# A batch-wise order for VectorE, a 32x32 q sketch with the Gram-weighted columns and FFN groups cut to batch 0, in a polysketch attention and FFN kernel

## The chip, the cores and the metric

One core of a Trainium2 chip. The metric is the device time of one launch in microseconds (us). Before the change the median is 131.13 us (four runs, 130.19 to 131.8). A run is called slow when it is over 1.5% above the fastest run of the same kernel. Ratios use fast runs alone; medians are over all runs.

## The reference, cut to what matters

```python
# q, k, v: (B, H, S, D) = (4, 4, 1088, 32); S1, S2: (8, 32)
phi(x) = outer(S1 x, S2 x)                   # 8 x 8 = 64 features per token and head
kv  = sum_s phi(k)_f v_d;  z = sum_s phi(k)_f
x   = (phi(q) kv) / (phi(q) z + 1e-6)        # 4352 tokens x 128 (heads side by side)
h   = x @ w_in                               # 128 -> 2048
out = (h - tanh(h)) @ w_out                  # 2048 -> 128
```

The FFN needs 160 tiles of tanh (16 per group of up to 512 columns) on ScalarE, and two matmuls per tile on TensorE. Columns are tokens; a batch has 1088 of them. `h @ w_out` without the tanh is folded into one small product, wc = w_in w_out (kept as wch + wcl). A sketch is the pair S1 x and S2 x. The denominator phi(q) z equals S1 q times G (S2 q), where G, the Gram matrix of a head, is the sum over tokens of the outer product of k's two sketches; G (S2 q) gives the Gram-weighted columns.

## The kernel before

A Python program lists operations with a key and their dependences; its own list scheduler models time and so fixes the order of instructions on every engine before the kernel is built.

```python
GCOLS = [256] + [512] * 7 + [384, 128]       # FFN groups: group 2 begins at column 768, inside batch 0
...
    # in schedule(): among what could start within 30 ns of the earliest, the lowest key wins
    t, o = min(((t, o) for t, o in cands if t <= t0 + 30.0), key=lambda x: (x[1].key, x[0]))
    ...
    st = max(t + 1400.0, dma_free)           # one model for all DMA queues
    dma_free = st + o.dma / 285.0
    o.t1 = dma_free + 600.0
...
    # q_side(): the key of a q transpose comes from when its columns are due, not from its batch
    P.add(_v((z - a) * 32), ... e.transpose(qT...), key=max(key, col_time(b * S + a * 32) - 9000) - 2000)
    # q sketch: S1 and S2 by 8 matmuls of 64x32, the Gram-weighted one by 4 of 128x32
    for g in range(4):
        for rh in range(2):
            e.matmul(psa4[g*32:(g+1)*32, rh, 0:sn], wab.ap[rh*64:(rh+1)*64, :], ...)
    ...                                       # two transposes back to abq
    e.matmul(psa4[g*32:(g+1)*32, 3, 0:sn], sc.ap[:, :], ...)
    ...                                       # one transpose back to cq
    # batch 0 in three sketches and pieces, the others in one sketch and two pieces
    q_side(b, sc, kvb, [(0, 2), (2, 5), (5, 9)], [(0, 2), (2, 5), (5, 9)], k0 + 5000)   # b == 0
    q_side(b, sc, kvb, [(0, 9)], [(0, 5), (5, 9)], kd + 6000)                            # others
```

Where the scheduler sees a long gap on TensorE early in the kernel, it puts filler matmuls on zeros there (line 367). Names on VectorE (DVE): kT and qT are 32x32-block transposes of loaded k and q; abk, abq, cq, abc bring a sketch back from PSUM; w and qp are the outer products; qpT transposes qp for the last attention product num; ot transposes an FFN group's output. The tiles psa, psh and pso are in PSUM, where the matmuls put their results; kvd and kvb are copies of the kv product out of PSUM, with a transpose on TensorE between them; xT is the attention's output, the FFN's input; th is a tile of tanh.

## Time and profile before

| view | what it shows |
|---|---|
| page, busy shares | PE 86%, ACT 65%, DVE 55% of a 130.5 us span |
| windows 50 to 104 us | PE busy 51.2 of 54 us |
| windows 104 to 127 us | ACT busy 22.8 of 23 us |
| windows 30 to 40 us | PE busy 2.6 of 10 us, ACT 0.8 |

The page's picture of the span in 40 slices (3.26 us each; a digit is a tenth busy):

```profile
PE   6998989674048899899899999999999999999990
DVE  5368678496934969963728982641997201002010
ACT  0315822751014269578587899659789999999990
PEclk9999999999855699999999999999999999999999
DMA  2999999999700000040000410400040130401322
```

The dip at 30 to 37 us is what the change aims at. The granted clock is 0.5 from 34.7 to 44.9 us; TensorE has no matmul from 30.97 to 37.12. The same stretch by windows (columns: stretch, its length, busy us and instructions of each engine, granted TensorE clock, DMA share, GB/s):

```profile
30.00:35.00 5.00, 0.83 (x25) 0.34 (x24) 3.90 (x11) 0.10 (x1) 0.00 (x0) 0.97 1.01 203
35.00:40.00 5.00, 1.76 (x72) 1.28 (x81) 2.07 (x4) 0.73 (x3) 0.00 (x0) 0.50 0.10 22
40.00:45.00 5.00, 4.53 (x62) 1.31 (x51) 3.93 (x7) 2.15 (x4) 0.00 (x0) 0.51 0.00 0
```

VectorE's timeline shows why TensorE starved (columns: start, us, engine, line, operation, tiles, count; in brackets the idle time before it and what ended it):

```profile
24.18 0.85 DVE L559 STREAM_TRANSPOSE qT<-qL 128x640 f32<-128x640 f32 x1 [1.02 <-DMA qL<-in_q_dram]
25.77 0.65 DVE L559 STREAM_TRANSPOSE qT<-qL 128x448 f32<-128x448 f32 x1 [0.64 <-DMA qL<-in_q_dram]
...
32.15 0.85 DVE L559 STREAM_TRANSPOSE qT<-qL 128x640 f32<-128x640 f32 x1 [0.73 <-DMA qL<-in_q_dram]
32.92 0.25 DVE L598 TENSOR_TENSOR m<-abq,cq 128x128 f32<-128x128 f32 x1
...
35.77 1.30 DVE L628 STREAM_TRANSPOSE qpT<-qp 128x512 f32<-128x512 f32 x2
```

These 640 and 448 wide qT are those of batches 1 and 2. Batch 0's last piece (m at 32.92, qpT at 35.77) stands behind a q load of batch 2 that landed at 32.1 us: VectorE idles 0.73 us for it, although m's last input, cq, was back at 31.42. ScalarE's timeline dates what follows:

```profile
38.68 0.59 ACT L318 CAST xT<-psa 128x384 bf16<-128x384 f32 x2 [8.59 <-PE psa L636]
39.86 0.60 ACT L702 ACTIVATE th<-psh 128x512 bf16<-128x512 f32 x1 [0.59 <-PE psa L636]
...
54.75 0.69 ACT L318 CAST xT<-psa 128x640 bf16<-128x640 f32 x1 [1.31 <-PE psa L636]
55.92 2.56 ACT L702 ACTIVATE th<-psh 128x512 bf16<-128x512 f32 x5 [0.48 <-PE psh L699]
```

FFN group 1 starts at 39.9 us, and group 2, which needs batch 1's first columns, at 55.9 us.

### The profile page before, as it was taken

How to read it: one execution, taken by the hardware profiler on the slowest of the kernel's cores; microseconds unless marked ns; L12 is line 12 of the kernel's file. 1: busy time of each engine (PE TensorE's matmuls, PEld its weight loads, DVE VectorE, ACT ScalarE, POOL GpSimd, SP SyncE). 2: the span in 40 equal slices, each digit the busy share in tenths (PEclk: the TensorE clock that was granted, in tenths of full speed). 3: DMA queues.
4: the chain of work that ended last, by engine and by line, in shares of the span. 5: the costliest groups of instructions: out<-in, count | busy, mean ns of one | idle time of the engine just before them, and what ended most of it. 6: DMA issues, size and time to landing. Idle time of an engine off the chain costs nothing.

```text
span 130.5 us, 3757 instructions
## 1 busy us (share of the span) xinstructions
PE 111.9 (86%) x1602; PEld 54.7 (42%) x1618; DVE 72.1 (55%) x155; ACT 85.2 (65%) x189; POOL 1.8 (1%) x14
## 2 busy tenths in 40 slices
PE   6998989674048899899899999999999999999990
PEld 4856656341022452333543444453335433334460
DVE  5368678496934969963728982641997201002010
ACT  0315822751014269578587899659789999999990
POOL 4100000000000000000000000000000000000000
PEclk9999999999855699999999999999999999999999
DMA  2999999999700000040000410400040130401322
GB/s 43 287 312 343 337 222 319 209 306 201 166 20 0 0 8 0 5 68 17 0 0 5 65 15 18 68 5 0 0 71 14 28 57 0 70 10 25 61 39 41
DMA packets 25552, 11.28 MB, mean 86 GB/s; under 512 B 19136, under 2 KB 24000, under 8 KB 25536
## 3 DMA queue, kind: packets, MB, share of 16 engines
q1 hardware_dynamic: 24528, 10.44, 35.4%
q10 hardware_dynamic: 1008, 0.61, 1.8%
q8 instruction: 12, 0.20, 0.7%
q14 instruction: 4, 0.03, 0.1%
HBM read 8.81 MB, written 2.23 MB: 85 GB/s over the span
## 4 chain that ended last, share of the span: by engine, by line
PE 48%; SPq 12%; DVE 12%; ACT 11%; DMA 11%; issue 3%
PE pso L712 16%; PE psh L699 16%; SPq L393 12%; DMA qL<-in_q_dram 11%; ACT th L702 10%; PE psa L636 6%; PE psa L532 3%; DVE w L522 3%; PE pso L716 2%; PE psa L491 2%; DVE abk L496 2%; DVE ot L721 1%; DVE qT L559 1%; PE psa L570 1%; ACT xT L318 1%
## 5 line engine op out<-in xcount | busy, mean ns | idle before, releaser
L702 ACT ACTIVATE th<-psh 128x512 bf16<-128x512 f32 (+3 forms) x160 | 72.0, 566 | 10.2 <-PE psh L699 9.3
L699 PE MATMUL psh<-xT,wi 128*128 128x512 bf16 (+3 forms) x152 | 51.9, 353 | 2.7 <-ACT th L702 1.2
L712 PE MATMUL pso<-th,wo 128*128 128x512 bf16 (+3 forms) x154 | 49.3, 349 | 1.1 <-issue 0.5
L699 PEld LDWEIGHTS psh<-xT,wi 128*128 128x128 bf16 x160 | 15.3, 98 | 24.2 <-ACT th L702 14.7
L712 PEld LDWEIGHTS pso<-th,wo 128*128 128x128 bf16 x160 | 15.3, 98 | 19.2 <-ACT th L702 7.0
L721 DVE STREAM_TRANSPOSE ot<-pso 128x512 f32<-128x512 f32 (+3 forms) x10 | 6.3, 635 | 25.7 <-PE pso L712 25.7
L636 PE MATMUL psa<-qpT,kvb 32*32 32x128 f32 (+3 forms) x576 | 10.1, 294 | 6.8 <-DVE qpT L628 6.8
L318 ACT CAST xT<-psa 128x384 bf16<-128x384 f32 (+3 forms) x11 | 5.1, 479 | 14.5 <-PE psa L636 14.5
L367 PE MATMUL pso<-zz 128*128 128x256 bf16 x86 | 12.6, 296 | 1.1 <-DVE zz L366 1.1
L628 DVE STREAM_TRANSPOSE qpT<-qp 128x512 f32<-128x512 f32 (+1 forms) x16 | 11.5, 755 | 0.1
L623 DVE TENSOR_TENSOR qp<-ap,abq 128x512 f32<-128x512 f32 (+1 forms) x16 | 11.3, 744 | 0.2
L522 DVE TENSOR_TENSOR w<-abk 128x768 f32<-128x768 f32 x12 | 11.1, 949 | 0.1
L636 PEld LDWEIGHTS psa<-qpT,kvb 32*32 32x32 f32 x576 | 6.6, 106 | 10.4 <-DVE qpT L628 7.5
L367 PEld LDWEIGHTS pso<-zz 128*128 128x128 bf16 x86 | 8.6, 106 | 3.2 <-DVE zz L366 1.1
L496 DVE STREAM_TRANSPOSE abk<-psa 128x288 f32<-128x288 f32 x8 | 3.4, 459 | 8.1 <-PE psa L491 8.1
L559 DVE STREAM_TRANSPOSE qT<-qL 128x448 f32<-128x448 f32 (+3 forms) x9 | 6.1, 673 | 2.9 <-DMA qL<-in_q_dram 2.9
L532 PE MATMUL psa<-w,vL 128*32 128x64 f32 x288 | 6.5, 223 | 1.2 <-DVE w L522 1.2
L575 DVE STREAM_TRANSPOSE abq<-psa 128x288 f32<-128x288 f32 (+3 forms) x12 | 3.9, 359 | 6.3 <-PE psa L570 6.3
L485 DVE STREAM_TRANSPOSE kT<-kL 128x576 f32<-128x576 f32 (+1 forms) x8 | 5.6, 718 | 3.1 <-DMA kL<-in_k_dram 3.1
L532 PEld LDWEIGHTS psa<-w,vL 128*32 128x32 f32 x288 | 4.7, 110 | 4.2 <-DVE w L522 3.6
L662 ACT CAST wi<-wi_f 128x512 bf16<-128x512 f32 x4 | 2.5, 620 | 4.5 <-DMA wi_f<-in_moe_w_in_dram 4.3
L491 PE MATMUL psa<-kT,wab 64*32 64x288 f32 x64 | 3.4, 481 | 1.3 <-ACT xT L318 1.1
(54 smaller groups left out, 59.1 us busy)
## 6 DMA issues: line engine op xcount, KB each, us to landing
kL<-in_k_dram SPq DMA_DIRECT2D x3, 544.0 KB, 11.9
vL<-in_v_dram SPq DMA_DIRECT2D x9, 144.0 KB, 12.5
wi_f<-in_moe_w_in_dram SPq DMA_DIRECT2D x4, 256.0 KB, 6.2
wo_f<-in_moe_w_out_dram SPq DMA_DIRECT2D x4, 256.0 KB, 7.2
out_dram<-ot SPq DMA_DIRECT2D x16, 64.0 KB, 2.0
qL<-in_q_dram SPq DMA_DIRECT2D x3, 320.0 KB, 13.8
qL<-in_q_dram SPq DMA_DIRECT2D x4, 224.0 KB, 12.7
vL<-in_v_dram ACTq DMA_DIRECT2D x3, 144.0 KB, 3.9
```

Of the source, the lines that this page charges most:

```text
L367: filler = (lambda e, n: e.matmul(bank_o.slots[0][0][:, 0:256], zz.ap[:, 0:128], zz.ap[:, 128:384], start=True, stop=True), zop, bank_o)
L393: return P.add({eng: (430.0, 0.0)}, lambda e, n: e.dma_start(out=o_, in_=i_), w=w, key=key, dma=nbytes)
L522: P.add(_v(768), lambda e, n, p=p, wv=wv: e.tensor_tensor(out=wv.ap.rearrange("p (x i j) -> p x i j", i=8, j=8), in0=abh()[:, 0, p * 12:(p ...
L532: i = e.matmul(psa4[h * 32:(h + 1) * 32, 2, 0:64], vL[b][:, h, blk * 32:(blk + 1) * 32], wv.ap[:, (bi * 4 + h) * 64:(bi * 4 + h + 1) * 64] ...
L559: P.add(_v((z - a) * 32), lambda e, n, a=a, z=z: e.transpose(qT.ap[:, a * 32:z * 32], qL[b][:, a * 32:z * 32]), r=[val], w=[qT], key=max(k ...
L623: P.add(_v(cn * 256), lambda e, n, aq=aq, qp=qp, av=av, c0=c0, c1=c1, cn=cn: e.tensor_tensor(out=qp.ap[:, 0:cn * 256].rearrange("p (x i j) ...
L628: P.add(_v(cn * 256), lambda e, n, qp=qp, qt=qt, c0=c0, c1=c1, cn=cn: e.transpose(qt.ap[:, c0 * 256:c1 * 256], qp.ap[:, 0:cn * 256]), r=[q ...
L636: i = e.matmul(psa4[h * 32:(h + 1) * 32, g, 0:nb * 32], kvb.ap[g * 32:(g + 1) * 32, x, h * 32:(h + 1) * 32], qq[g * 32:(g + 1) * 32, 0:nb, ...
L699: P.add(_pe(n_ / 2.4 + 2.6), lambda e, n, jb=jb, hv=hv: e.matmul(hv.ap[:, 0:n_], wi[jb // 4].ap[:, (jb % 4) * 128:(jb % 4 + 1) * 128], xt, ...
L702: P.add(_a(n_), lambda e, n, hv=hv, th=th: e.activation(out=th.ap[:, 0:n_], in_=hv.ap[:, 0:n_], func=AF.Tanh, scale=-1.0), r=[hv], w=[th], ...
L712: fn = lambda e, n, x=x, st=st, sp_=sp_: e.matmul(ov.ap[:, 0:n_], wo[x // 4].ap[:, x % 4, :], ths[x].ap[:, 0:n_], start=st, stop=sp_)
L721: P.add(_vp(n_), lambda e, n: e.transpose(ot.ap[:, 0:n_], ov.ap[:, 0:n_]), r=[ov], w=[ot], key=-60000)
```

## The change

The intent is that a piece of batch 0 never stands behind work of a later batch on VectorE, with fewer and larger VectorE instructions in the q sketch, and FFN groups cut so that the first three need batch 0 alone. The core of the diff, with cuts:

```diff
-GCOLS = [256] + [512] * 7 + [384, 128]
+GCOLS = [256, 384, 448] + [512] * 6 + [192]
+WINDOW = {"tensor": 60.0, "vector": 150.0, "scalar": 60.0, "gpsimd": 30.0, "sync": 30.0}
 ...
-                t, o = min(((t, o) for t, o in cands if t <= t0 + 30.0), key=...)
+                t, o = min(((t, o) for t, o in cands if t <= t0 + WINDOW[e]), key=...)
 ...
-                st = max(t + 1400.0, dma_free)
-                dma_free = st + o.dma / 285.0
-                o.t1 = dma_free + 600.0
+                st = max(t + 1400.0, dma_free.get(e, 0.0))        # a model per issuing queue
+                dma_free[e] = st + o.dma
+                o.t1 = dma_free[e] + (600.0 if o.key < -89800 else 2000.0)
 ...
-    qcut = {0: [0, 8, 20, 34]}                                    # others [0, 20, 34]
+    qcut = {0: [0, 8, 34]}                                        # others whole
 ...
+    def nk():                                                     # attention keys: program order
+        seq[0] += 1
+        return -50000.0 + seq[0]
 ...
+            for h in range(H):                                    # q sketch: S1 | S2 | Gram-weighted S2
+                for g in range(4):
+                    i = e.matmul(psa4[g * 32:(g + 1) * 32, h, 0:sn], wq[h * 32:(h + 1) * 32, :],
+                                 qv4(b)[h * 32:(h + 1) * 32, s0:s1, g, :], start=True, stop=True)
+        P.add(_pe(sn * 4 / 2.4 + 100), sk, ..., w=bk, key=nk(), mode="32x32")   # all four psa banks
+        P.add(_vp(sn * 4), ... e.transpose(abc ...), r=bk, w=[abc], key=nk())   # one, in place of three
 ...
-                after=[])
+                after=[last], name=f"wc{jb}")                     # wc waits for the last wo cast
 ...
-    for b in range(B):
-        kd = k0 if b == 0 else col_time(b * S) - 16500.0
-        sc, kvb = k_side(b, kd)
-        ...
+    attention_first()                                             # batch 0: sketches (0,2) and (2,9)
+    weights()
+    for b in range(1, B):
+        k_side(b)
+        st = q_front(b)                                           # one sketch, one divide per batch
+        q_back(b, st)
```

Also moved: the PSUM copies gm, sc, kvd, kvb and xT are ScalarE's alone; one wi cast and three wo casts went to GpSimd; the ring of tanh tiles has 24 slots in place of 28.

## The prediction

> **What bounds it now.** The windows show three stages.
> - 0 to 40 us: attention of batch 0, behind DMA and VectorE. From 30 to 40 us TensorE is busy 2.6 of 10 us. VectorE's timeline shows why: it runs in order, and transposes of later batches' q stand ahead of batch 0's last q piece (qT at 24.18, 25.77, 32.15 us, each after a DMA wait). Its xT copy comes at 38.7 us, the first 512-column FFN group's tanh at 39.9. TensorE's clock is 0.5 from 34.7 to 44.9 us.[...]
> - 40 to 104 us: TensorE, busy 9.1 to 9.6 of each 10 us after 50. Group 2 (columns 768 on) waits for batch 1's first xT copy and starts tanh at 55.9.
> - 104 to 127 us: ScalarE, 60 tanh back to back (23.7 us), then a tail of 3.3 us.
>
> **What the change does.**
> 1. VectorE order: batch 0's q pieces no longer stand behind later q. Batch 1's kT still stands ahead of batch 0's second abc; its load landed at 20.5 us and the bytes ahead of it are the same, so VectorE starts again there.
> 2. q sketch: 8 matmuls 64x32 (0.73 us) and 4 of 128x32 (0.65) become 16 in 32x32, estimate 0.8: TensorE saves 0.6 us a batch. Three VectorE transposes (0.85 + 0.44 us) become one of 1152 columns (estimate 1.35): equal. One divide per batch instead of two saves about 0.6 us.
> 3. gm, kvd, kvb, xT all go to ScalarE (0.2 to 0.7 us each); it has room in the middle.
> 4. FFN groups 256, 384, 448 cover batch 0's 1088 columns, so batch 1 is first needed at 1088 instead of 768.
> 5. wo casts mostly on GpSimd; all wc matmuls wait for the last. wo3 landed at 18.0, so group 0 starts near 20.5, before 22.3.
>
> **Timeline expected** (old durations and landings). VectorE from 20.5: kT 0.7, abc 1.1, wcl and divide 1.8, qp and qpT: batch 0 done at 29 (was 37.1). Then kT, qT, abk, w, more kT and qT, abc, divide and five blocks of batch 1, 16.5 us without a DMA wait: 45.7. num 1.2, xT 0.7: group 3 (column 1088) starts near 48. Groups 1 and 2 fill 27 to 43 at ScalarE's pace; ScalarE then waits 5 us, TensorE about 2.5[...].
> From there the old trace is the measure: group 2 started at 55.9 with 3584 columns, batches 2 and 3 and one piece of batch 1 left, and ended (ot) at 127.9: 72.0 us. The new one has 320 columns less (34 matmuls of 0.2155 us per 512: 4.6 us) and 1.2 us less sketch: 66.2. 48 + 66.2 + 2.6 (output) = 116.8; timed runs lie some 0.4 above the profile.
>
> **Predicted: 117 us, 80% between 112 and 122.** Faster by over 2%: 0.95; within 2%: 0.04; slower: 0.01.
>
> **Signs.** Right: num of batch 0's last piece by 30 us instead of 37; no 0.5 clock between 20 and 100 us; group 3 tanh at 46 to 50 us; the ScalarE-bound end near 21 us. Wrong: VectorE waiting for kL or qL after 21 us; ScalarE held by wch.
>
> **What would make it wrong.** [...]kL or wo3 landing later, loads being cut and ordered differently; slow GpSimd casts; or VectorE faster than summed, the gap shrinking (-3 us).

The estimates in it can be followed from the profile before: 512-column matmuls start 0.216 us apart; transposes of 448 and 640 columns take 0.63 and 0.84 us, by which 1152 come to about 1.4; num's 32 matmuls of 32x32 (64 records) take 1.07 us with 128 columns and 1.18 with 160, by which 16 with 288 come to about 0.8 (this last is my reckoning; the record does not say from what 0.8 was taken). The divide of a later batch (m, den, rd, ap) took 2.23 us in two pieces before and takes 1.75 in one after, so it saves 0.5 where 0.6 was forecast.

## The result, and the profile after

| | before | after |
|---|---|---|
| median, us | 131.13 (130.19 to 131.8, 4 runs) | 123.83 (122.75 to 124.78, 4 runs) |
| profiled span, us | 130.5 | 122.6 |
| PE / ACT busy, us | 111.9 / 85.2 | 107.0 / 85.9 |
| first tanh of groups 1, 2, 3 | 39.9, 55.9, 67.8 | 31.8, 43.3, 53.6 |
| first group that needs batch 1 | group 2 (from column 768) | group 3 (from column 1088) |

The ratio is 0.942 (0.9324 to 0.9516). Ratios here are the mean time of one kernel's fast runs over that of the other's fast runs of the same rounds, so not quite the ratio of the medians quoted. The kernel is faster by 7.3 us, where 14 were forecast, and lies above the range of 112 to 122. Both profiled runs were slow ones (132.3 us, a run outside these four, and 124.78 us), so the two profiles are compared like with like.

The page after, same lines (slices of 3.07 us):

```profile
PE   6995696849859999969999999989999999989980
DVE  5529480895738999984908992662999020020210
ACT  0402661746737789777788898838988998989970
PEclk9999679985999999999999999999999999999999
DMA  1999999999991004022000310050005005004052
```

The hole at 30 to 37 us is gone. In its place are smaller dips, and two short falls of the clock, at 13.2 to 16.7 and 26.9 to 30.3 us. By windows:

```profile
25.00:30.00 5.00, 3.41 (x47) 2.21 (x47) 4.08 (x6) 2.92 (x9) 0.00 (x0) 0.69 1.05 230
30.00:35.00 5.00, 3.53 (x114) 1.73 (x82) 3.49 (x5) 2.50 (x6) 0.00 (x0) 0.97 1.07 228
35.00:40.00 5.00, 4.85 (x104) 2.32 (x104) 2.71 (x5) 3.25 (x10) 0.00 (x0) 1.00 0.42 96
```

VectorE's timeline, from the load it waits for to group 3's input:

```profile
21.80 0.78 DVE L502 STREAM_TRANSPOSE kT<-kL 128x576 f32<-128x576 f32 x1 [3.82 <-DMA kL<-in_k_dram]
...
31.39 0.45 DVE L781 STREAM_TRANSPOSE ot<-pso 128x256 f32<-128x256 f32 x1 [2.21 <-PE pso L772]
31.77 0.67 DVE L653 STREAM_TRANSPOSE qpT<-qp 128x512 f32<-128x512 f32 x1
...
37.26 0.85 DVE L513 STREAM_TRANSPOSE abk<-psa 128x288 f32<-128x288 f32 x2 [2.38 <-PE psa L522]
...
44.17 1.38 DVE L610 STREAM_TRANSPOSE abc<-psa 128x1152 f32<-128x1152 f32 x1 [0.26 <-PE psa L605]
```

No DMA wait stands in it after 21.8 us, as forecast. But twice VectorE waits over 2 us for TensorE. ScalarE's timeline then has group 3:

```profile
52.46 0.69 ACT L319 CAST xT<-psa 128x640 bf16<-128x640 f32 x1 [1.20 <-PE psa L662]
53.63 1.58 ACT L762 ACTIVATE th<-psh 128x512 bf16<-128x512 f32 x3 [0.48 <-PE pso L772]
```

Why is TensorE late? Its timeline shows two gaps that no semaphore explains:

```profile
24.84 0.28 PE L759 MATMUL psh<-xT,wi 128*128 128x256 bf16 x1
26.72 0.28 PE L772 MATMUL pso<-th,wo 128*128 128x256 bf16 x1 [1.59 <-issue]
...
32.97 0.87 PE L662 MATMUL psa<-qpT,kvb 32*32 32x128 f32 x40
35.10 0.48 PE L662 MATMUL psa<-qpT,kvb 32*32 32x128 f32 x24 [1.26 <-issue]
```

"issue" means that the engine waited for nothing that the profile shows. The second gap lies inside one operation, num, of 64 matmuls on the same operands, all of them ready: 40 run, the engine stops, and 24 follow.

**Where these gaps lie.** If one counts all of TensorE's records in order of start (matmuls, weight loads and 17 records of semaphores and drains, 7 of which come before the first gap), the gaps end at records 705 and 961. These are 256 apart. The page lists a DMA queue of its own for instructions, here after and before in turn:

```profile
q8 instruction: 13, 0.21, 0.7%
```

```profile
q8 instruction: 12, 0.20, 0.7%
```

Each of these packets has 16,384 bytes, and TensorE has 3,245 records (1616 matmuls and 1629 weight loads), or 12.7 times 256. That the packets are TensorE's, and that each brings its next 256 records, is inferred from this count and from the times below; the trace names neither the engine nor the moment at which a packet is asked for. Delays are therefore counted from the record at which the block before begins (first column), worked out from the packets of that queue and the records:

```text
kernel after: block begins  | next block's packet starts, done | its first record runs
record 449 at 18.60         | 23.88 (5.3 us later), 25.17      | record  705 at 26.71 (gap 1.87)
record 705 at 26.71         | 32.16 (5.5 us later), 33.62      | record  961 at 35.10 (gap 1.53)
record 961 at 35.10         | 36.74 (1.6 us later), 37.84      | record 1217 at 40.33 (no gap)
record 1217 at 40.33        | 41.05 (0.7 us later), 42.32      | record 1473 at 51.35 (no gap)
```

(A gap here is from the start of one record to the start of the next.) The last input load lands at 39.4 us. For the first two rows, with many loads still queued, the packet starts more than 5 us after the block before began, and TensorE resumes 1.5 us after it is done; for the third, near the end of the loads, it starts 1.6 us after. From record 449 to 705 it is 8.1 us, from there to 961 another 8.4.

### The profile page after: what moved, and what is told of

It is laid out like the page before. It is cut to its first block, busy times and chain, and to the rows that moved or that the text cites. A ratio compares the mean times of both kernels' runs of the same rounds, so it can differ in the third digit from the quotient of the medians.

```text
span 122.6 us, 3742 instructions
## 1 busy us (share of the span) xinstructions
PE 107.0 (87%) x1616; PEld 52.6 (43%) x1629; DVE 68.7 (56%) x110; ACT 85.9 (70%) x197; POOL 4.8 (4%) x24
## 3 DMA queue, kind: packets, MB, share of 16 engines
HBM read 8.81 MB, written 2.23 MB: 90 GB/s over the span
## 4 chain that ended last, share of the span: by engine, by line
PE 57%; DVE 12%; SPq 8%; DMA 8%; issue 6%; ACT 5%; DVEq 0%
PE pso L772 22%; PE psh L759 19%; SPq L397 8%; DMA kL<-in_k_dram 8%; PE psa L662 7%; ACT th L762 5%; DVE w L555 4%; PE psa L568 3%; DVE ot L781 3%; PE pso L776 2%; DVE abc L610 2%; PE psa L605 2%; DVE abk L513 2%; PE psa L522 2%; DVE kT L502 1%
## 5 line engine op out<-in xcount | busy, mean ns | idle before, releaser
L762 ACT ACTIVATE th<-psh 128x512 bf16<-128x512 f32 (+4 forms) x160 | 72.9, 561 | 13.1 <-PE psh L759 11.5
L759 PE MATMUL psh<-xT,wi 128*128 128x512 bf16 (+4 forms) x153 | 52.8, 355 | 2.7 <-ACT xT L319 0.7
L772 PE MATMUL pso<-th,wo 128*128 128x512 bf16 (+4 forms) x154 | 49.0, 354 | 3.0 <-issue 2.2
L781 DVE STREAM_TRANSPOSE ot<-pso 128x512 f32<-128x512 f32 (+4 forms) x10 | 6.2, 621 | 24.7 <-PE pso L772 24.7
L648 DVE TENSOR_TENSOR qp<-ap,abc 128x512 f32<-128x512 f32 (+1 forms) x16 | 11.7, 730 | 0.2
L368 PE MATMUL pso<-zz 128*128 128x256 bf16 x57 | 9.8, 337 | 1.1 <-DVE zz L367 1.1
L610 DVE STREAM_TRANSPOSE abc<-psa 128x1152 f32<-128x1152 f32 (+2 forms) x5 | 5.7, 1134 | 8.7 <-PE psa L605 8.7
L368 PEld LDWEIGHTS pso<-zz 128*128 128x128 bf16 x57 | 6.5, 121 | 3.4 <-DVE zz L367 1.1
L509 DVE STREAM_TRANSPOSE qT<-qL 128x1088 f32<-128x1088 f32 (+2 forms) x5 | 5.3, 1051 | 1.4 <-DMA qL<-in_q_dram 1.4
L605 PE MATMUL psa<-qT,wq 32*32 32x288 f32 (+2 forms) x160 | 3.5, 381 | 1.5 <-ACT wq L547 1.5
```

The lines of the kernel that those rows point to most:

```text
L368: filler = (lambda e, n: e.matmul(bank_o.slots[0][0][:, 0:256], zz.ap[:, 0:128], zz.ap[:, 128:384], start=True, stop=True), zop, bank_o)
L610: P.add(_vp(sn * 4), lambda e, n: e.transpose(abc.ap.rearrange("p k h f -> p h k f")[:, :, 0:s1 - s0, :], psa4[:, :, 0:sn].rearrange("p h ...
L648: P.add(_v(cn * 256), lambda e, n, qp=qp, c0=c0, cn=cn: e.tensor_tensor(out=qp.ap[:, 0:cn * 256].rearrange("p (x i j) -> p x i j", i=8, j= ...
L759: P.add(_pe(n_ / 2.4 + 2.6), lambda e, n, jb=jb, hv=hv: e.matmul(hv.ap[:, 0:n_], wi[jb // 4].ap[:, (jb % 4) * 128:(jb % 4 + 1) * 128], xt, ...
L762: P.add(_a(n_), lambda e, n, hv=hv, th=th: e.activation(out=th.ap[:, 0:n_], in_=hv.ap[:, 0:n_], func=AF.Tanh, scale=-1.0), r=[hv], w=[th], ...
L772: fn = lambda e, n, x=x, st=st, sp_=sp_: e.matmul(ov.ap[:, 0:n_], wo[x // 4].ap[:, x % 4, :], ths[x].ap[:, 0:n_], start=st, stop=sp_)
```

## The experiments

Sixteen kernels ran, all correct. Theory (A in the expectations, the reading of the 256 records and the packets above): TensorE stops at the ends of blocks of 256 records because the next block's packet is late behind the input loads. (A clause on how instructions come is cut from the expectation of a1, where it stood as fact and not as this inference; from those of a3, b1, d3 and e2, what names the moment at which a fetch is asked for, which no trace shows. A delay here is from the start of the block before.) Rivals: VectorE's own order (an output transpose ahead of qpT, later k and q transposes) makes the chain late and TensorE with it; or the groups and sketch cost more than thought. Medians are over all runs; "before" ran at 131.36 to 131.53 us beside them. The profiles of the first and third kernels of call 1, the window, c1 and c2 of call 2 and d2 of call 3 are of slow runs, so group starts and gaps read from them are not those of the fast runs that give the ratios.

### Call 1: where the stall lies, and VectorE's order

Two filler matmuls of 128 columns for one of 256, which puts 114 more records ahead of the stretch in question:

```diff
-filler = one matmul of 256 columns
+filler = two matmuls of 128 columns each
```

> The changed kernel, each idle-time filler matmul of 256 columns split into two of 128: same TensorE time, 57 more matmuls and 57 more weight loads (about 114 records more before the tanh groups begin). Theory A (TensorE runs dry of instructions[...]): the two stalls that the chain calls issue, 1.6 us at record 705 and 1.3 us at record 961, stay at records 705 and 961 (within 5), that is 114 records earlier in the program (the q sketch of the second part, and the first matmuls of group 1), and the first gets longer, 2 to 4 us; time 0.5 to 3 us above the changed kernel. Theory B (the stall belongs to its place: a wait for data that the profile doesn't show): the stalls stay at group 0's o matmul and inside the num of batch 0's last piece, records 819 and 1075, time the same.

Measured: 122.63 us, ratio 0.9252 (0.9154 to 0.9349). The gaps are at records 961 (0.85 us) and 1217 (3.44 us, from 34.98 to 38.42); the one at 705 is gone. Group 3 starts at 54.7. So the gap keeps its record number modulo 256 and leaves the instructions that it hit before. I had expected it to be slower, which it was not, and I had the wrong block end for the long gap. Its two fast runs, 122.03 and 120.75 us, even lie below the three of the kernel after (122.75 to 124.05, another set), which the slow profile cannot explain.

One filler of 512 columns for two of 256, so fewer records:

```diff
-while t + 110.0 + 200.0 < b:      # one 256-column filler each 110 ns
+while t + 220.0 + 200.0 < b:      # one 512-column filler each 220 ns
```

> The changed kernel, two fillers of 256 columns made one of 512: same TensorE time, about 58 records fewer. Theory A: the stall at record 705 moves 58 records later in the program, is met later in time, and shrinks from 1.6 us to under 0.8; then no half clock from 27 to 30 us; group 3's first tanh 1.5 to 3.5 us earlier than 53.6, time 1 to 3 us below the changed kernel. Theory B: nothing moves, time within 0.5 us.

Measured: 124.84 us, 0.9488 (0.94 to 0.9576), group 3 at 53.3. Gaps of 1.89, 0.73 and 2.27 us at records 447, 703 and 959; the last is now in the k sketch. The hoped-for gain of 1 to 3 us did not come: the gaps move to other instructions, and their sum does not fall (4.9 us, against 3.4 in the kernel after).

The loads of batches 2 and 3 wait until batch 1's q has landed:

```diff
+    k_load[2].deps[q_load[1]] = True
```

> The changed kernel, the loads of batches 2 and 3 held until batch 1's q has landed (about 27 us), nothing else reordered. Theory A: the fetch for record 961[...] finds only a short queue: it starts within 2 us instead of 5.4, and the stall of 1.3 us at record 961 is gone; group 3 0.7 to 2 us earlier, unless kT of batch 2, which stands ahead of abk in VectorE's order, waits for its load (then a DMA wait of VectorE at about 32 to 34 us, and the gain is lost). The stall at record 705 stays, since batch 1's loads are still under way. Theory B: both stalls stay.

Measured: 123.1 us, 0.9261 (0.9181 to 0.9342). While few loads were queued, the packet of the block for record 961 began 2.1 us after the block before did, in place of 5.5, and that gap is gone. Then the held loads run together, until 39 us, and the gap is at record 1217 (1.90 us). Group 3 at 53.4. The link between queued loads and the late packet holds in both directions. In the slow profiled run nothing is gained; the two fast runs, 121.4 and 121.63 us, are below those of the kernel after, so whether holding gains time is left open, the sets being different.

The first output transpose behind batch 0's last qpT on VectorE:

```diff
+    move("vector", ["ot0"], behind="qpT0.5")
```

> The changed kernel, group 0's output transpose moved behind batch 0's last qpT on VectorE. Theory C (VectorE's order is what delays group 3: the 2.2 us wait for group 0 in front of the last qpT): qpT 2.6 us earlier, group 3 earlier by 1.5 us or more, time 1 to 2 us less. Theory A (TensorE, starved and half-clocked, is late with group 0 and reaches the num of the last piece only at about 33 us whatever VectorE does): qpT earlier, that num at most 0.5 us earlier, time within 0.5 us.

Measured: 123.53 us, 0.9401 (0.9327 to 0.9476). The last qpT of batch 0 starts at 28.0 in place of 31.8 us, but xT of that piece is at 35.12 (35.73 after), as the gaps (2.49 and 1.63 us) hold TensorE. Group 3 at 53.0. The output transpose was thus not what made the chain late, although it is the line that shows the wait.

### Call 2: a bounded load queue, and parts of the change

A load on the sync queue is issued only when those further back than the last 768 KB have landed:

```diff
+    for i in range(6, len(mine)):          # mine: the loads of the sync queue in order
+        room = 768 * 1024
+        for j in range(i - 1, -1, -1):
+            room -= mine[j][1]
+            if room <= 0:
+                mine[i][0].deps[mine[j][0]] = True
+                break
```

> The changed kernel with a window on the loads of the sync queue: from the second wi load on, a load is issued only when the loads before the last 768 KB have landed; engine orders unchanged. Theory A1 (an instruction fetch of TensorE waits behind the loads already queued; the four runs before had 3.2 to 4.9 us of stall in total wherever the block ends fell): [...]stalls at block ends (records 193 + 256 k) sum to under 1.5 us between 15 and 40 us, group 3's first tanh at 50 to 52 us instead of 53.0 to 54.6, time 1 to 4 us below the changed kernel; if the window starves the loads, the last q lands after 41 us instead of 39.4 and part of it is lost. Theory A2 (only the total traffic counts, not how much is queued): stalls still sum to 3 us or more, time within 1 us.

Measured: 120.97 us (fast runs 120.73 to 121.21), 0.9218 (0.914 to 0.9296). Packets begin 0.6 to 1.4 us after the block before did; after 15 us the only gap at a block end is one of 0.37 us, and the clock is full from 17.6 us on. Windows of this kernel, against those of after above:

```profile
25.00:30.00 5.00, 4.69 (x92) 2.45 (x92) 4.79 (x9) 3.63 (x12) 0.00 (x0) 1.00 0.70 230
30.00:35.00 5.00, 4.74 (x97) 2.21 (x97) 4.40 (x8) 3.90 (x11) 0.00 (x0) 1.00 0.35 94
```

TensorE is busy 9.4 us of these 10 in place of 6.9. From 25 to 30 us the DMA moves 230 GB/s in both kernels, so the rate of bytes alone does not make the packet late (the DMA engines' busy share, though, is 0.70 against 1.05). Group 3 starts at 52.1 only, because now loads are late: VectorE waits 1.7 us for batch 3's k, which stands ahead of batch 1's abc.

VectorE's k and q transposes put behind the earlier batch's last qpT, and wc later on TensorE, without and with the window:

```diff
+    move("vector", ["ot0"], "qpT0.5")
+    move("vector", ["kT1.0", "kT1.1", "qT1.0"], "qpT0.5")
+    move("vector", ["kT2.0", "kT2.1", "qT2.0", "kT3.0", "kT3.1"], "qpT1.5")
+    move("vector", ["wcl"], "aq0.2"); move("tensor", wc, "h0.4"); move("scalar", ["wch"], "th0.4")
```

> The changed kernel, orders alone: batch 1's k and q transposes behind batch 0's last qpT, batches 2 and 3's behind batch 1's; the wc matmuls (which wait for the last wo cast) behind group 0's fifth h instead of ahead of the q sketch, wch and wcl moved to fit; output transpose 0 behind them. Theory V (VectorE's waits for kL and for TensorE in front of batch 0's second part are what is left to gain): abc of batch 0's second part at 19 to 20 us instead of 22.5, its last qpT at 26 to 27 instead of 32.4, group 3's first tanh at 47 to 49 us. Theory A (TensorE's instruction supply paces the load phase: about 256 records per 8 us): batch 0 may finish early, but stalls at block ends stay 3 us or more and group 3 starts no earlier than 51 us; time at most 2 us below the changed kernel.

> Both of the last two: the new orders and the load window. If A1 and V are both right the gains add: group 3 at 44 to 48 us, time 116 to 120 us. If only one is right, it is like the better of the two alone (within 1 us).

Measured: 126.72 us, 0.9576 (0.9456 to 0.9696), and 126.27 us (one fast run, so no ratio). My edit was faulty: the lines were moved in an order that left ot0 behind kT1 and qT1, where it was to be ahead of them. The first is slower than after in its fast runs too (124.98 and 126.18 us); the one fast run of the second, 123.59, is within after's. They say nothing on the theory but this: with the window there was again no gap of over 0.5 us at a block end after 15 us, and without it one of 1.67 us.

The kernel before with only the change's scheduler windows and DMA model; the work is as before and the instructions are ordered anew:

```diff
+WINDOW = {"tensor": 60.0, "vector": 150.0, ...}
-                dma_free = st + o.dma / 285.0
+                dma_free[e] = st + o.dma          # per queue, own rates
```

> The kernel before, with the change's load model and choice windows in its scheduler and nothing else: the order of VectorE changes (batch 2's q transposes now stand behind batch 0's last q piece), old sketch, old groups, old cuts. If the order alone is what the change gains (theory O): 1 to 3 us of the 7.4 lie in the groups and sketch, this kernel is at 124 to 127 us, and the half clock from 34.7 to 44.9 us is gone or shorter. If the groups matter as much (theory G: batch 1 first needed at column 1088 instead of 768): 127 to 130 us.

Measured: 127.9 us, 0.977 (0.9663 to 0.9877). Group 1 starts at 36.9 (39.9 before), group 2 at 50.5 (55.9). A better order of the old work is worth some 3 us (2.9 by the means of fast runs; the interval lies below 1, though at 2% the verdict is unclear).

### Call 3: the mended order, a smaller window, the old groups

```diff
+    move("vector", ["kT1.0", "kT1.1", "qT1.0"], "qpT0.5")
+    move("vector", ["ot0"], "qpT0.5")             # now ahead of them
+    move("vector", ["qT2.0", "kT3.0", "kT3.1"], "qpT1.5")
+    move("vector", ["kT2.0", "kT2.1"], "qpT1.0")  # wcl, wc, wch as in c2
```

> The new orders and the load window again, with the fault of the first try mended: output transpose 0 directly behind batch 0's last qpT (it stood behind three more transposes, and group 1's o matmuls waited for it), kT of batch 2 behind batch 1's first piece. If the wait for TensorE's instructions and VectorE's order were the two terms missing from the forecast, they add: group 1's first tanh at 28 to 30 us, abk of batch 1 at 31 to 33, group 3's first tanh at 44 to 47 us directly behind group 2, time 114 to 118 us. If something else paces the first 45 us, group 3 stays at 50 us or later and the time at 120 or more.

> The mended orders without the load window. Theory A1: stalls at block ends (records 193 + 256 k) of 3 us or more in total after 15 us, group 3 2 to 4 us later than in the run with the window: 47 to 50 us, time 118 to 121 us. If the window is worth nothing once the order is right: within 1 us of the run with both.

Measured with the window: 122.64 us (122.34 to 123.46), 0.9357 (0.9312 to 0.9401); group 3 at 50.5, where 44 to 47 was expected. VectorE of this kernel:

```profile
35.04 2.69 DVE L558 TENSOR_TENSOR w<-abk 128x768 f32<-128x768 f32 x3
41.06 1.38 DVE L613 STREAM_TRANSPOSE abc<-psa 128x1152 f32<-128x1152 f32 x1 [3.33 <-PE psa L608]
```

With its other work moved away, VectorE is idle for 3.3 us: the new q sketch writes all four psa banks, so it must wait until the kv product in one of them has gone through kvd (38.43 us), its transpose (38.95) and kvb (39.59) on ScalarE and TensorE; the sketch starts at 40.11. The moved transposes had only filled that wait. They come later instead: group 4 starts at 64.2, as it does with the window alone (64.3). Without the window: 126.24 us, one fast run, gaps of 0.89 and 3.05 us, group 3 at 54.0. The time was to be 114 to 118 us with the window and 118 to 121 without. The one fast run without it, 123.14 us, lies within the range with it, so here the gaps differ and the time is not shown to; the mended order on top of the window does not pay.

The same with a window of 512 KB:

> The mended orders with a window of 512 KB. If less queued is always better for the fetches: [...]stalls at most as with 768 KB. But the window also slows the loads (the last q landed at 47.4 us with 768 KB against 39.4 without): with 512 KB later than 50 us, and weights and batch 1 1 to 3 us later. I expect 0 to 3 us above the run with 768 KB.

Measured: 124.97 us, 0.9501 (0.9425 to 0.9577). No gap of over 0.5 us at a block end after 15 us, but the last q lands at 53.6 us and group 3 starts at 52.3: a window too small pays in late loads what it saves in gaps.

The kernel after with the old FFN groups:

```diff
-GCOLS = [256, 384, 448] + [512] * 6 + [192]
+GCOLS = [256] + [512] * 7 + [384, 128]
```

> The changed kernel with the old FFN groups (256, seven of 512, 384, 128). Theory G (groups that end with batch 0 are worth something, since batch 1 is first needed at column 1088): group 1 (columns 256 to 768) needs both pieces of batch 0 and starts at 35 to 37 us instead of 31.8, group 2 waits for batch 1 (about 53 us), so at the time group 3 starts now, 320 columns (4.6 us of TensorE) less are done: time 126 to 129 us. Theory O (order alone): within 1 us of the changed kernel.

Measured: 131.68 us (131.56 to 131.75), 1.0039 (0.9986 to 1.0091), where 126 to 129 was expected: all of the gain is gone. ScalarE's timeline:

```profile
33.12 0.59 ACT L319 CAST xT<-psa 128x384 bf16<-128x384 f32 x2 [4.60 <-PE psa L662]
34.08 0.60 ACT L762 ACTIVATE th<-psh 128x512 bf16<-128x512 f32 x1 [0.37 <-PE psh L759]
...
51.77 0.69 ACT L319 CAST xT<-psa 128x640 bf16<-128x640 f32 x1 [5.22 <-PE psa L662]
53.16 1.08 ACT L762 ACTIVATE th<-psh 128x512 bf16<-128x512 f32 x2 [0.70 <-PE psh L759]
```

Batch 1's columns come at the same time as after (51.77 and 52.46 us), but without groups 1 and 2 both fed from batch 0, TensorE and ScalarE run dry at 46.5 us and the clock halves from 51.0 to 57.8. The groups have their worth in filling the time of batch 1's chain, and in this order the earlier start of batch 0 is worth nothing without them. (The old work ordered anew, above, did gain with the old groups: there batch 1's group starts at 50.5 us, here at 53.2.) No run has the new groups with the old sketch and order, so what the sketch is worth by itself is not shown.

### Call 4: the cause, in one set on one chip, five rounds each

The unaltered kernel after; a control in which batch 3's kT stands behind batch 1's last qpT; that with the window of 768 KB; and that with 1024 KB.

```diff
+    move("vector", ["kT3.0", "kT3.1"], "qpT1.5")     # e0, e1, e2
+    room = 768 * 1024                                # e1; 1024 * 1024 in e2; no window in e0
```

> The changed kernel once more, unaltered, on the chip of the next three: 122.5 to 125 us, stalls at block ends of 3 us or more after 15 us, group 3 at 52.5 to 54.5 us. If it comes out under 122 us, the gain of the load window is mostly a difference of chips.

> Control: the changed kernel with kT of batch 3 behind batch 1's last qpT, no load window. VectorE waits there for TensorE, not for the load, so nothing is gained: within 1 us of the unaltered kernel, stalls as there.

> The window of 768 KB with kT of batch 3 behind batch 1's last qpT. VectorE's wait for batch 3's k in front of abc of batch 1 (1.7 us) is gone, abc at 41 to 41.5 us instead of 42.7, group 3 at 50 to 51 us instead of 52.1; time 119 to 120.5 us against about 121. If group 3 comes earlier and the time doesn't, a later chain (batch 2's abk, at 56.1 us) paces from there.

> The same with a window of 1024 KB: loads a little faster (last q at 43 to 46 us instead of 47.4)[...]; within 1 us of the window of 768 KB. More than 2 us slower would say that the stalls set in sharply between the two.

| kernel | median, us | ratio to before | gaps of over 0.5 us at block ends | group 3 | last q lands |
|---|---|---|---|---|---|
| after again | 124.46 (123.03 to 125.31) | 0.9411 (0.9339 to 0.9483) | 1.56, 2.50 | 53.5 | 37.0 |
| kT3 moved | 124.22 (123.43 to 124.93) | 0.9467 (0.9406 to 0.9528) | 1.82, 2.23 | 52.4 | 37.0 |
| kT3 moved, 768 KB | 121.75 (120.48 to 123.4) | 0.9247 (0.918 to 0.9313) | none | 51.1 | 44.1 |
| kT3 moved, 1024 KB | 120.67 (119.96 to 122.31) | 0.9198 (0.9143 to 0.9254) | none | 50.2 | 40.4 |

Gaps are counted after 15 us. The same operation, num of batch 0's last piece, in the chains of waits of the unaltered kernel and of the one with 1024 KB (columns: start, us, what):

```profile
30.58 0.80 PE psa L662 x40
31.38 2.24 issue
33.62 0.48 PE psa L662 x24
```

```profile
31.18 1.00 PE psa L665 x56
```

In the second it runs without a break. Moving kT3 alone gains nothing in time; the window takes away the gaps and 3.6 us from that control's median (124.22 to 120.67; the intervals of the ratios do not meet). This last version has the lowest median seen: 10.9 us below before's of the same set (131.53), though not clear of the window alone (120.97). With 768 KB the time missed the expected 119 to 120.5 us, so moving kT3 is not shown to save time on top of the window; with 1024 KB the last q landed earlier than the 43 to 46 us expected.

## Why the prediction was right or wrong

The mechanism held as far as it went: batch 0's pieces no longer stand behind later q loads on VectorE (batch 1's k load still comes ahead of one, as forecast), the hole at 30 to 37 us closed, and the kernel is faster (with the new groups; with the old ones this order gained nothing). What it left out made the size wrong. The sum against the trace, in us:

| term | forecast | measured | off by |
|---|---|---|---|
| VectorE restarts on batch 1's k load | 20.5 | 21.8 | +1.3 |
| from there to batch 0's last qpT done | 8.5 (to 29) | 10.6 (to 32.4) | +2.1 |
| from there to batch 1's five qpT done | 16.7 (to 45.7) | 18.7 (to 51.1) | +2.0 |
| num, xT, first tanh of group 3 | 2.3 (to 48) | 2.5 (to 53.6) | +0.2 |
| group 3 to the last ot done | 66.2 | 65.9 | -0.3 |
| output | 2.6 | 3.0 | +0.4 |
| median over the profiled span | 0.4 | 1.2 | +0.8 |

- **The term that failed is "48", group 3's start.** Of its 5.6 us, 4.1 are in the two VectorE rows. The prediction summed VectorE's own durations and called the rest "16.5 us without a DMA wait". That was true, but it left out the waits for TensorE: 2.21 us in front of batch 0's last qpT and 2.38 us in front of abk. I had taken TensorE to be free whenever its inputs were there. The sign, num of batch 0's last piece by 30 us, came at 33.0.
- **TensorE was not free, because its instructions were late** (the inference above). In eleven of the twelve kernels without the load window, 21 gaps of over 0.5 us (0.7 to 3.4) after 15 us lie at these block ends, and each ends 1.3 to 1.7 us after the late packet is done, which began 3.7 to 6.9 us after the block before did. (In the twelfth, the old work in the new order, there is none.) In the six kernels with a window there is none. The kernel before has one too, of 1.16 us at record 705 (23.55 to 24.71 us), labelled as a wait for ScalarE, so I read over it.
- **The other part is the clock.** "No 0.5 clock between 20 and 100 us" was wrong: it was 0.5 from 26.9 to 30.3 us. The pairs of 256-column matmuls run 0.43 us apart then, against 0.28 at full clock in the 1024 KB version. Over the five pairs of that stretch (27.19 to 29.32 us) this is some 0.7 us, an estimate from these steps. The half-clock stretch is 3.41 us long. In the 3.41 us before it, in which the gap of 1.87 us wholly lies, TensorE was busy 1.50 us; before the twelve falls between 20 us and the end of the work, in eleven of the kernels, it was busy 0 to 1.83 of such a stretch, while four stretches of 3.4 us in the control (22.2 to 35.8 us) had 1.95 to 2.99 and no fall. What sets the clock is not shown by this. How the loss divides between gaps and clock in the timed runs is not separated.
- **kL landing later** was named as a risk and came in part: 21.8 us here, but 20.8 in the same kernel's other profile, which reached group 3 no earlier (53.5).
- **Group 3 on was right.** In after, its repeat, the control, the window alone and the two windows of call 4, the span less group 3's start is 68.9 to 69.1 us. So what these versions gain, they gain at that start. The ScalarE-bound end is about 21 us long, as forecast (tanh nearly without pause from 97 to 119).
- **The sizes were right**: 1152-column transpose 1.38 us (1.35 estimated); the 32x32 sketch about 0.78 us (0.8); a wo cast takes 0.61 to 0.63 us on GpSimd and 0.62 on ScalarE. Group 0 starts at 21.9 (20.5 was forecast and 22.3 was before): GpSimd waits for the last wo load until 19.7, which was to land at 18.0. wch did not hold ScalarE.
- **The median's offset** was small in the forecast because the slow profiled run of before was set beside a median of faster runs. Within one run of after the time is 2.1 to 2.2 us above the span. Its profile too was of its slowest run (124.78), so its median lies 1.2 above that span.

With the window group 3 starts at 50.2 us, 2.2 above the 48: k lands at 22.4 us, and TensorE's bank chain ahead of abc keeps VectorE waiting 1.5 us. So at that start the window is worth 3.3 us against the unaltered kernel of this set, whose profile also has half clock from 35.0 to 38.4 us, and 2.2 us against the control, whose profile has none then. Open is why a packet on a queue of its own is late behind the loads on other queues: the runs show that it follows the loads' depth, not the mechanism, and whether the packet waits or is asked for late is not in the trace. Open too is why the block ends fall at 193 modulo 256 in my count.

## What to carry to other kernels

When a forecast is a sum along one engine, add the waits for the other engines, and where a profile says "issue" or a wait that its releaser cannot explain, look at where in the engine's own instruction stream it falls. Keep the queue of loads only as deep as they are needed: here 1024 KB in flight in place of everything at once gained 3.6 us of the median with the same bytes, and 512 KB (with a changed order) was too little. Recut consumers together with producers: in this order the earlier batch 0 gained nothing until the FFN groups were cut to its 1088 columns.
